# Squared-ReLU attention with a mixture of experts: x's upper parts read in place, whole-pair turns, and a new order of the work around each chunk

## The chip, the cores and the metric

One Trainium2 chip, one of its cores. The time is device microseconds of one launch of the whole program. Engines are called as the profile calls them: PE (TensorE matmuls), PEld (TensorE weight loads), DVE (VectorE), ACT (ScalarE), POOL (GpSimd), SP (SyncE, which issues nearly all DMAs).

## The reference

```python
# u, v: (8, 2496, 256), z: (8, 2496, 64), all float32
attn = np.maximum(z @ z.transpose(0, 2, 1) / 2496, 0.0) ** 2
x = (u * (attn @ v)).reshape(19968, 256)

logits = x @ w_gate                       # 8 experts
expert_idx = np.argmax(logits, axis=1)
probs = np.exp(logits - logits.max(-1, keepdims=True))
probs /= probs.sum(-1, keepdims=True) + 1e-09
gate_w = probs[np.arange(N), expert_idx]
for e in range(8):
    tok_idx = np.where(expert_idx == e)[0]      # at most 80 kept, by gate_w
    h = np.maximum(x[tok_idx] @ w1[e], 0.0)     # 256 -> 1024
    out[tok_idx] = gate_w[tok_idx, None] * (h @ w2[e])
```

The scores are symmetric, so that a block of attn can also be had as the transpose of another one.

## The kernel before

The sequence of each batch is cut into five chunks of 512 queries (the last has 448) and into ten pairs of 128-key tiles. A step is one pair of keys against one chunk of queries: 8 batches x 5 chunks x 10 steps. The loop over steps is written out by hand, and every engine works its own instructions strictly in the order in which the program issues them.

In step r the program issues, in this order: the scores of the pair two steps ahead (`scores`, 6 matmuls L401 into the PSUM tile `s`, of which there is one; then ACT's ReLU L403 out of `s` and ACT's square L404 into the tile `a`, of which there are two); the attention matmuls of the present pair (`attend_pair`, 24 matmuls L439 into `acc`; at step 9 ACT copies the two finished halves of `acc` out, `take` L508); the split of the pair two steps ahead (`split`: an upper part `ah`, cast on ACT L114 or on DVE L116, and a rest `al`, a DVE subtraction reported at the helper's line L58; then DVE turns the pair in blocks of 32 x 32, `mirror` L309, for the mirrored block, which goes out to DRAM as `y` and comes back as `blk`). Where the key block lies before the chunk, no scores are computed: `mirrored` casts `blk` on ACT (L381) and subtracts on DVE. So chunk 0 computes all its ten pairs, and chunk 4 nearly none. The pair on the diagonal is computed by half and turned into `xd` (L346), written as `yd` and read back as `md`.

`acc` has two tiles, one for each half of the 256 columns, and the next chunk's step 0 writes them again.

The finished chunk (`prev`) is worked on during the steps of the next one, in `finished(*prev, r)`. At step 0, `chunk_x` on DVE adds the two halves of the sum and scales them with u (L513). Then x is split into three bf16 parts for the gate's logits: `chunk_hi` (step 1, an ACT cast L518 into `xb`), `chunk_rest` (step 2, DVE), `chunk_mid` (step 3, an ACT cast L526), `chunk_lo` (step 4, DVE). `chunk_store` writes x at step 3 or 4, and `chunk_logits` at step 6 or 7 has 48 small matmuls (L598), each with its weight load out of `xb`; `chunk_sum` adds up their results at the same step. After a batch's last chunk, `gate_top` (step 8: DVE, with the one Exp on ACT, L629, in its middle) and `gate_near` and `gate_sum` (step 9) run in chunk 0 of the next batch.

v is loaded two tiles ahead (`vraw`, two buffers) and split as x is, the upper part by an ACT cast L114 and the rest by a DVE subtraction L143, for the next batch's tiles 0 to 3 at steps 1, 3, 6 and 8 of chunk 4, and for tile 4 at step 3 of the next chunk 0. Weights for the experts come in during the last batch. Behind the last step stands the experts' part.

SP's queue is in program order too. Among its DMAs are `ut` (L150, one buffer, issued at step 2, so that it waits for `chunk_x` of the chunk before), `vraw` (L131), `y`, `blk`, `md`, `xu` (x, L577) and zeros for `out`.

Of the kernel before, what the change touches and what calls it, by code (L numbers as in the profile page):

```python
# [19 lines left out]
P = 128  # L20
# [5 lines left out]
def attn_moe_kernel(ctx, tc, zT, uT, v, wg, w1, w2, out, seq, cap):  # L26
# [15 lines left out]
    QT = 4  # L42
# [83 lines left out]
    def load_v(b, g):  # L126
        last = g == NQ - 1
        nf = QT - 1 if last else QT
        raw = zpool.tile([P, QT, D], F32, tag="vraw", name=f"vraw_{b}_{g}")
        r0 = g * CH  # L130
        nc.sync.dma_start(out=raw[:, :nf],  # L131
                          in_=v[RB[b], r0:r0 + nf * P, :].rearrange("(t p) d -> p t d", p=P))
        if last:

            r1 = r0 + nf * P
            for h in range(2):
                nc.sync.dma_start(out=raw[h * 64:(h + 1) * 64, nf], in_=v[RB[b], r1:r1 + TAIL, :])
        return raw

    def prep_v(b, g, raw, e0, e1):  # L140
        vt = vpool.tile([P, QT, 2, D], F32R, tag="vt", name=f"vt_{b}_{g}")
        cp(e0, vt[:, :, 0], raw)
        e1.tensor_tensor(out=vt[:, :, 1], in0=raw, in1=vt[:, :, 0], op=ALU.subtract)  # L143
        v_t[b, g] = vt

# [357 lines left out]
    def take(b, qc, c):  # L503
# [68 lines left out]
    def chunk_store(b, qc):  # L572
# [37 lines left out]
    def gate_top(b, q0, q1):  # L610
# [363 lines left out]
    def finished(b, qc, r):  # L974

        at_end = b == B - 1 and qc == NQ - 2
        if r == 1:
            chunk_hi(b, qc)
        if r == (1 if at_end else 2):
            chunk_rest(b, qc)  # L980
        if r == (2 if at_end else 3):
            chunk_mid(b, qc)
        if r == (3 if at_end else 4):
            chunk_lo(b, qc)
        if r == (3 if at_end or b >= 2 else 4):
            chunk_store(b, qc)
        if r == (5 if at_end else 6):
            chunk_store2(b, qc)
        if r == (5 if at_end else 6 if qc == NQ - 1 else 7):
            chunk_logits(b, qc)  # L990
            chunk_sum(b, qc)
        if b < B - 1 and qc == NQ - 1:
            if r == 8:
                gate_top(b, 0, NQ)
            elif r == 9:
                gate_sum(b, gate_near(b, 0), gp)
        elif qc == 0 and b > 0:
            if r == 5:
                count(b - 1, 0, BPB, b - 1)
# [3 lines left out]
        elif at_end and r == 7:  # L1003
            gate_top(b, 0, NQ - 1)

    with tc.manual_schedule(engines={ET.PE, ET.Activation, ET.DVE, ET.SP, ET.Pool}):
# [10 lines left out]
        for i, (b, qc, r) in enumerate(steps):  # L1017
# [33 lines left out]
            nb, nqc = (b, qc + 1) if qc + 1 < NQ else (b + 1, 0)  # L1051
            if r == 2:
                prep_u(b, qc)
            if b + 1 < B:
                for j, load, prep in keys_in[qc]:
                    if r == prep:
                        prep_z(b + 1, j, z_raw.pop((b + 1, j)))
                    if r == load:
                        z_raw[b + 1, j] = load_z(b + 1, j)
                if qc == NQ - 2 and r in (2, 4):  # L1060
                    g = r // 2 - 1
                    v_raw[b + 1, g] = load_v(b + 1, g)
                if qc == NQ - 1:
                    if r in (1, 3, 6, 8):
                        g = (1, 3, 6, 8).index(r)
                        prep_v(b + 1, g, v_raw.pop((b + 1, g)), nc.scalar, V)
                        if g + 2 < NQ:
                            v_raw[b + 1, g + 2] = load_v(b + 1, g + 2)
# [490 lines left out]
```

## Time and profile before

| | us |
|---|---|
| Time, median of 3 runs | 1420.04 |
| Lowest and highest | 1419.43 and 1427.58 |
| The profiled execution's own time | 1427.79 |
| Its span, first to last instruction | 1426.1 |

The profiled execution is thus one of the longer ones: 7.75 us above the median, and 1.7 us of it lie around the span. Mean granted TensorE clock: 0.985 of full speed. Busy shares of the span: PE 93%, PEld 76%, DVE 78%, ACT 73%, POOL 3%. A busy time is the union of an engine's instructions; the matmuls' ends are modelled, so that a busy PE can still be a PE at half clock.

### The profile page before, as it was taken

What the parts mean: (1) busy time and instruction counts of PE and PEld (TensorE: products, weight loads), DVE (VectorE), ACT (ScalarE), POOL (GpSimd) and SP (SyncE); (2) the same over time, 40 slices, a digit from 0 to 9 for tenths busy, and PEclk for the clock granted to TensorE, in tenths of its full rate; (3) what the DMA queues carried; (4) which work ended last, traced back from release to release, by engine and by line L of the source; (5) the groups of instructions that cost most, each with busy time, mean ns of one, the idle gap of its engine ahead of it and who ended that gap; (6) DMA issues with size and microseconds to landing.
All of it is one profiled execution on the core that took longest, in us unless ns stands there. A gap on an engine that the chain in (4) does not pass through costs nothing.

```text
span 1426.1 us, 31554 instructions
## 1 busy us (share of the span) xinstructions
PE 1332.9 (93%) x13121; PEld 1086.2 (76%) x13121; DVE 1113.1 (78%) x1531; ACT 1036.0 (73%) x1124; POOL 38.9 (3%) x58
## 2 busy tenths in 40 slices
PE   9999989999899988999999998999999998899997
PEld 6788767887777877878778776787777787787776
DVE  8887788768878788877878678876887768777785
ACT  8875777847777577766877577784777757777765
POOL 0000000000001000000002000000000000000111
PEclk9999999999999999999999999999999999999999
DMA  6898786995878856887567857787479685578764
GB/s 214 275 278 234 219 240 200 234 270 152 234 217 234 235 161 224 228 237 211 190 203 216 244 154 227 213 232 215 137 222 269 188 224 172 189 223 243 196 223 134
DMA packets 192744, 307.02 MB, mean 215 GB/s; under 512 B 35873, under 2 KB 117713, under 8 KB 182353
## 3 DMA queue, kind: packets, MB, share of 16 engines
q1 hardware_dynamic: 191312, 302.62, 72.6%
q0 software_dynamic: 1280, 2.30, 0.6%
q8 instruction: 105, 1.72, 0.5%
q14 instruction: 47, 0.38, 0.1%
HBM read 163.66 MB, written 136.09 MB: 210 GB/s over the span
## 4 chain that ended last, share of the span: by engine, by line
PE 41%; ACT 20%; DVE 17%; DMA 11%; issue 7%; SPq 3%; DVEq 0%; ACTq 0%; POOL 0%; POOLq 0%
PE acc L439 31%; DVE al L58 6%; PE s L401 5%; ACT a L403 5%; ACT a L404 4%; DMA blk<-y 4%; ACT ah L114 3%; DVE x L309 3%; DVE xf L58 3%; DMA y<-x 2%; ACT xf L508 2%; ACT ah L381 2%; PE hp L1286 2%; ACT vt L114 2%; DVE xf L513 1%
## 5 line engine op out<-in xcount | busy, mean ns | idle before, releaser
L439 PE MATMUL acc<-ah,vt 64*128 64x512 f32 (+1 forms) x6240 | 969.3, 387 | 19.8 <-ACT xf L508 19.0
L439 PEld LDWEIGHTS acc<-ah,vt 64*128 64x128 f32 x6240 | 597.6, 186 | 135.1 <-ACT xf L508 30.3
L439 PE MATMUL acc<-al,vt 64*128 64x512 f32 (+1 forms) x3120 | 624.7, 390 | 31.1 <-DVE al L58 30.2
L439 PEld LDWEIGHTS acc<-al,vt 64*128 64x128 f32 x3120 | 305.6, 186 | 105.8 <-DVE al L58 53.2
L58 DVE TENSOR_TENSOR al<-a,ah 128x1024 fp32r<-128x1024 f32 (+1 forms) x240 | 271.8, 1132 | 125.6 <-ACT ah L114 120.5
L403 ACT ACTIVATE a<-s 128x1024 f32<-128x1024 f32 x240 | 229.0, 954 | 120.5 <-PE s L401 117.5
L58 DVE TENSOR_TENSOR al<-blk,ah 128x1024 fp32r<-128x1024 f32 x160 | 193.2, 1219 | 86.3 <-ACT ah L381 86.3
L404 ACT ACTIVATE a<-a 128x1024 f32<-128x1024 f32 x240 | 238.0, 992 | 7.6
L309 DVE STREAM_TRANSPOSE x<-a 128x512 f32<-128x512 f32 x320 | 207.7, 687 | 0.0
L381 ACT CAST ah<-blk 128x1024 fp32r<-128x1024 f32 x160 | 161.2, 1048 | 22.8 <-PE acc L439 12.7
L114 ACT CAST ah<-a 128x1024 fp32r<-128x1024 f32 x153 | 161.0, 1052 | 4.4
L518 ACT CAST xb<-xf 128x1024 bf16<-128x1024 f32 (+1 forms) x39 | 40.1, 1027 | 103.8 <-DVE xf L513 103.5
L508 ACT COPY xf<-acc 128x1024 f32<-128x1024 f32 (+1 forms) x78 | 75.0, 991 | 34.0 <-PE acc L439 32.0
L401 PE MATMUL s<-zh,zh 64*128 64x512 f32 x320 | 66.8, 414 | 28.0 <-ACT a L403 28.0
L401 PE MATMUL s<-zh,zl 64*128 64x512 f32 x480 | 90.3, 372 | 0.0
L401 PE MATMUL s<-zl,zh 64*128 64x512 f32 x480 | 90.0, 370 | 0.0
L116 DVE CAST ah<-a 128x1024 fp32r<-128x1024 f32 (+3 forms) x87 | 49.3, 567 | 34.9 <-ACT a L404 34.6
L401 PEld LDWEIGHTS s<-zh,zh 64*128 64x128 f32 x320 | 30.4, 186 | 44.5 <-ACT a L403 39.4
L526 ACT CAST xb<-xf 128x1024 bf16<-128x1024 f32 (+1 forms) x39 | 40.0, 1026 | 29.3 <-DVE xf L58 29.2
L143 DVE TENSOR_TENSOR vt<-vraw,vt 128x1024 fp32r<-128x1024 f32 x40 | 48.2, 1204 | 13.4 <-ACT vt L114 13.4
L401 PEld LDWEIGHTS s<-zl,zh 64*128 64x128 f32 x480 | 45.6, 185 | 8.3
L401 PEld LDWEIGHTS s<-zh,zl 64*128 64x128 f32 x480 | 45.8, 186 | 5.7
(188 smaller groups left out, 856.3 us busy)
## 6 DMA issues: line engine op xcount, KB each, us to landing
y<-x SPq DMA_DIRECT2D x80, 1024.0 KB
blk<-y SPq DMA_DIRECT2D x320, 256.0 KB
out<-idle SPq DMA_DIRECT2D x40, 512.0 KB
vraw<-v SPq DMA_DIRECT2D x32, 512.0 KB
ut<-uT SPq DMA_DIRECT2D x32, 512.0 KB
wraw<-w SPq DMA_DIRECT2D x30, 512.0 KB
xu<-xf SPq DMA_DIRECT2D x24, 512.0 KB
yd<-xd SPq DMA_DIRECT2D x37, 256.0 KB
```

The source lines that it names most:

```text
L58: V.tensor_tensor(out=o, in0=a, in1=b, op=op)
L114: eng.copy(out=o, in_=i)
L116: eng.tensor_copy(out=o, in_=i)
L143: e1.tensor_tensor(out=vt[:, :, 1], in0=raw, in1=vt[:, :, 0], op=ALU.subtract)
L309: V.transpose(out=x[:, :, :, t].rearrange("p n k s -> p k n s"), in_=a)
L381: nc.scalar.copy(out=natural(ah), in_=src)
L401: nc.tensor.matmul(s[:, h, c0:c1], zk[hs, t * P:(t + 1) * P], zq[hs], start=n == 0, stop=n == 2)
L403: nc.scalar.activation(out=a[:, :, c0:c1], in_=s[:, :, c0:c1], func=AF.Relu)
L404: nc.scalar.activation(out=a[:, :, c0:c1], in_=a[:, :, c0:c1], func=AF.Square)
L439: nc.tensor.matmul(acc_t[b, qc][c][:, h, :nq], v_t[b, k // QT][hs, k % QT, iv, c * P:(c + 1) * P], x[hs, k % 2, :nq], start=at not in begu ...
L508: nc.scalar.copy(out=x[:, :, c], in_=acc_t[b, qc][c][:, :, :x.shape[-1]])
L518: nc.scalar.copy(out=xb[:, 0], in_=xf)
```

## The change

- x's upper parts are no longer cast. A float32 read as two bf16 has its upper half at every second place; `top(x)` is that view. The logits' weight loads and the two subtractions `chunk_rest` and `chunk_lo` read it with a step of two. `chunk_hi` and `chunk_mid` are gone; of the tile `xb` only the third part stays (`xl`).
- `chunk_x` is cut in two: the addition stays at step 0, the scaling moves to step 1 (not in the last chunk). `chunk_rest`, `chunk_lo`, store, rows, logits and sum go to steps 3, 5, 4, 6, 7 and 9 (8 behind a batch's last chunk).
- DVE turns a whole pair (1024 columns) in one instruction in place of two of 512; the diagonal's quarter likewise in one of 512 in place of two of 256.
- The diagonal pairs' casts move from DVE to ACT, except in chunk 0 of each batch.
- `gate_top` moves to step 9 of chunk 0, without the Exp; Exp goes to step 0 of chunk 1, `gate_near` to step 2, the row sums and the reciprocal to step 3, and their four DMAs to step 5.
- v is loaded at steps 2, 3, 5 and 9 of chunk 3 and step 6 of chunk 4, into three buffers; it is cast at step 6 of chunk 3 and steps 3, 5, 7 and 9 of chunk 4, and each subtraction follows one step behind.
- `ut` is loaded at step 4 in place of step 2.

```diff
-    def prep_v(b, g, raw, e0, e1):
+    def prep_vh(b, g, raw, e0):
         vt = vpool.tile([P, QT, 2, D], F32R, tag="vt", name=f"vt_{b}_{g}")
         cp(e0, vt[:, :, 0], raw)
+        v_t[b, g] = vt
+
+    def prep_vl(b, g, raw, e1):
+        vt = v_t[b, g]
         e1.tensor_tensor(out=vt[:, :, 1], in0=raw, in1=vt[:, :, 0], op=ALU.subtract)
...
-        V.transpose(out=x[:, :, :, t].rearrange("p n k s -> p k n s"), in_=a)
-        if t < QT - 1:
+        V.transpose(out=x[:, :, :, t:t + 2].rearrange("p n k t s -> p t k n s"), in_=a)
+        if t < QT - 2:
             return
...
-        on_v = k // QT == qc or (qc, k) in ON_V and b > 0
+        on_v = k // QT == qc and qc == 0 or (qc, k) in ON_V and b > 0
...
+    def top(x):
+        return x.bitcast(BF16)[..., 1::2]
+
     def chunk_tiles(b, qc):
         xf = xpool.tile([P, 2, DC, CH], F32, tag="xf", name=f"xf_{b}_{qc}")
-        xb = xpool.tile([P, 3, DC, CH], BF16, tag="xb", name=f"xb_{b}_{qc}")
+        xl = xpool.tile([P, DC, CH], BF16, tag="xl", name=f"xl_{b}_{qc}")
...
+    def chunk_add(b, qc):
+        x = x_sum[b, qc]
+        tt(x[:, 0], x[:, 0], x[:, 1], ALU.add)
+
     def chunk_x(b, qc):
         x = x_sum.pop((b, qc))
-        tt(x[:, 0], x[:, 0], x[:, 1], ALU.add)
         V.scalar_tensor_tensor(out=x[:, 0], in0=x[:, 0], scalar=CSQ, in1=u_t[b, qc][:, :, :x.shape[-1]],
                                op0=ALU.mult, op1=ALU.mult)
 
-    def chunk_hi(b, qc):
-        xf, xb, _ = xt_t[b, qc]
-        nc.scalar.copy(out=xb[:, 0], in_=xf)
-
     def chunk_rest(b, qc):
-        xf, xb, xr = xt_t[b, qc]
-        tt(xr, xf, xb[:, 0], ALU.subtract)
-
-    def chunk_mid(b, qc):
-        _, xb, xr = xt_t[b, qc]
-        nc.scalar.copy(out=xb[:, 1], in_=xr)
+        xf, xr, _ = xt_t[b, qc]
+        tt(xr, xf, top(xf), ALU.subtract)
 
     def chunk_lo(b, qc):
-        _, xb, xr = xt_t[b, qc]
-        tt(xb[:, 2], xr, xb[:, 1], ALU.subtract)
+        _, xr, xl = xt_t[b, qc]
+        tt(xl, xr, top(xr), ALU.subtract)
...
-                    nc.tensor.matmul(to[:, h, t], xb[hs, i % 3, i // 3, t0:t0 + P], wgs[hs, i // 3],
+                    nc.tensor.matmul(to[:, h, t], xb[i % 3][hs, i // 3, t0:t0 + P], wgs[hs, i // 3],
                                      start=i == 0, stop=i == 3 * DC - 1)
...
+    V_LOAD = [(NQ - 2, 2), (NQ - 2, 3), (NQ - 2, 5), (NQ - 2, 9), (NQ - 1, 6)]
+    V_HIGH = [(NQ - 2, 6), *((NQ - 1, r) for r in (3, 5, 7, 9))]
...
-        if r == 1:
-            chunk_hi(b, qc)
-        if r == (1 if at_end else 2):
+        rest, lo, store, store2, logits, total = (1, 2, 3, 5, 5, 5) if at_end else CHAIN
+        if qc == NQ - 1:
+            logits, total = 7, 8
+        if r == rest:
             chunk_rest(b, qc)
-        if r == (2 if at_end else 3):
-            chunk_mid(b, qc)
...
-        if b < B - 1 and qc == NQ - 1:
-            if r == 8:
-                gate_top(b, 0, NQ)
-            elif r == 9:
-                gate_sum(b, gate_near(b, 0), gp)
+        if b < B - 1 and qc == NQ - 1 and r == 9:
+            gate_top(b, 0, NQ)
         elif qc == 0 and b > 0:
-            if r == 5:
+            if r == 0:
+                gate_exp(b - 1, 0)
+            elif r == 2:
+                ex_t[b - 1] = gate_near(b - 1, 0)
+            elif r == 3:
+                gate_rows(b - 1, ex_t.pop(b - 1), gp, V)
+                gate_recip(b - 1, gp)
+            elif r == 5:
+                gate_store(b - 1)
...
+    CHAIN = 3, 5, 4, 6, 7, 9
...
             if r == 0 and prev:
+                chunk_add(*prev)
+            if r == (0 if last else 1) and prev:
                 chunk_x(*prev)
...
-            if r == 2:
+            if r == 4:
                 prep_u(b, qc)
...
-            if b and qc == 0 and r == 3:
-                prep_v(b, NQ - 1, v_raw.pop((b, NQ - 1)), nc.scalar, V)
+                if (qc, r) in V_HIGH:
+                    g = V_HIGH.index((qc, r))
+                    prep_vh(b + 1, g, v_raw[b + 1, g], nc.scalar)
+            v_low(b, qc, r)
```

## Rows read from the trace of the kernel before

**Rows 1.** Windows, chunks 0, 2, 3: us, PE, PEld, DVE, ACT, POOL, clock, DMA.

```profile
681.83:720.11 38.28, 33.30 (x330) 26.50 (x330) 31.09 (x44) 29.87 (x33) 0.00 (x0) 1.00 0.67 216
...
755.35:787.67 32.32, 32.25 (x328) 26.23 (x328) 25.71 (x42) 25.67 (x27) 10.10 (x8) 1.00 0.79 211
787.67:821.11 33.44, 31.04 (x300) 24.63 (x300) 22.07 (x26) 17.96 (x21) 0.00 (x0) 0.95 0.87 249
```

**Rows 2.** The waits view, whole run: us in total, times, longest us.

```profile
ACT a L403 <- PE s L401: 117.5, 78, 4.0
ACT xb L518 <- DVE xf L513: 103.5, 36, 4.1
...
PE acc L439 <- DVE al L58: 30.2, 40, 2.4
PE s L401 <- ACT a L403: 29.7, 28, 1.5
...
PE acc L439 <- ACT xf L508: 19.0, 16, 2.4
```

**Rows 3.** The timeline of PE in batches 4 and 5: waits in brackets.

```profile
693.31 0.50 PE L401 MATMUL s<-zh,zh 64*128 64x512 f32 x2 [1.48 <-ACT a L403]
...
720.27 0.73 PE L439 MATMUL acc<-ah,vt 64*128 64x512 f32 x4 [2.14 <-ACT xf L508]
...
798.77 0.50 PE L439 MATMUL acc<-al,vt 64*128 64x512 f32 x2 [2.38 <-DVE al L58]
...
837.94 0.47 PE L439 MATMUL acc<-al,vt 64*128 64x448 f32 x2 [0.42 <-DVE al L58]
...
853.99 0.40 PE L401 MATMUL s<-zh,zh 64*128 64x512 f32 x2
```

**Rows 4.** The timeline of ACT in batches 4 and 5.

```profile
691.40 0.94 ACT L518 CAST xb<-xf 128x896 bf16<-128x896 f32 x1 [2.59 <-DVE xf L513]
...
718.86 0.34 ACT L629 ACTIVATE lg<-d 128x160 f32<-128x160 f32 x1 [3.33 <-DVE d L58]
...
852.72 1.04 ACT L403 ACTIVATE a<-s 128x1024 f32<-128x1024 f32 x1
```

**Rows 5.** The timeline of DVE around the starts of chunks 1 and 3.

```profile
719.57 0.32 DVE L636 TENSOR_TENSOR oh<-fw,mf 128x160 bf16<-128x160 f32 x1
...
722.11 1.23 DVE L58 TENSOR_TENSOR al<-blk,ah 128x1024 fp32r<-128x1024 f32 x1 [2.09 <-ACT ah L381]
...
796.36 1.22 DVE L513 SCALAR_TENSOR_TENSOR xf<-xf,ut 128x1024 f32<-128x1024 f32 x1
797.50 1.22 DVE L58 TENSOR_TENSOR al<-blk,ah 128x1024 fp32r<-128x1024 f32 x1
```

**Rows 6.** Windows: first and last of nine at half clock, and one more.

```profile
120.90:124.31 3.41, 3.41 (x20) 2.69 (x18) 2.98 (x3) 1.93 (x3) 0.00 (x0) 0.50 0.94 328
...
1138.07:1141.48 3.41, 3.41 (x18) 2.67 (x16) 2.89 (x3) 1.93 (x3) 0.00 (x0) 0.50 0.95 326
693.00:697.00 4.00, 3.69 (x32) 3.07 (x34) 3.04 (x5) 3.90 (x5) 0.00 (x0) 1.00 0.92 344
```

**Rows 7.** The lines view by shape: count, busy us, mean ns, idle before.

```profile
L309 DVE STREAM_TRANSPOSE x<-a 128x512 f32<-128x512 f32 x320 | 207.7, 687 | 0.0
...
L114 ACT CAST ah<-a 128x1024 fp32r<-128x1024 f32 x153 | 161.0, 1052 | 4.4
...
L518 ACT CAST xb<-xf 128x1024 bf16<-128x1024 f32 x32 | 33.5, 1046 | 85.7 <-DVE xf L513 85.4
...
L116 DVE CAST ah<-a 128x1024 fp32r<-128x1024 f32 x41 | 28.5, 695 | 21.9 <-ACT a L404 21.7
```

**Rows 8.** The timeline of PEld around one chunk's logits: start us, us.

```profile
708.72 0.67 PEld L598 LDWEIGHTS <-xb 64*128 64x128 bf16 x48 [0.26 <-issue]
709.32 0.19 PEld L401 LDWEIGHTS s<-zh 64*128 64x128 f32 x2
709.42 0.19 PEld L401 LDWEIGHTS s<-zh,zl 64*128 64x128 f32 x2
```

More of the change, by code (lines that the diff above doesn't have):

```diff
@@ L128, in load_v @@
         nf = QT - 1 if last else QT
-        raw = zpool.tile([P, QT, D], F32, tag="vraw", name=f"vraw_{b}_{g}")
+        raw = zpool.tile([P, QT, D], F32, tag="vraw", name=f"vraw_{b}_{g}", bufs=3)
         r0 = g * CH
@@ L344, in quarter_out @@
         x = zpool.tile([P, n32, 2, 2, SQ], F32, tag="md", name=f"xd_{b}_{qc}", bufs=1)
-        for t in range(2):
-            V.transpose(out=x[:, :, :, t].rearrange("p n k s -> p k n s"), in_=a[:, t, HQ:])
+        V.transpose(out=x.rearrange("p n k t s -> p t k n s"), in_=a[:, :, HQ:])
         quarter[b, qc] = now[0], x
@@ L423, in split @@
         if k // QT > qc:
-            for h in range(2):
-                mirror(b, k // QT, qc, k % QT + h, a[:, h])
+            mirror(b, k // QT, qc, k % QT, a)
         a_t[b, qc, k] = (ah, al)
@@ L491, in attn_moe_kernel @@
     xt_t, xq_t, lg_t = {}, {}, {}
+    def top(x):
+        return x.bitcast(BF16)[..., 1::2]
     def chunk_tiles(b, qc):
         xf = xpool.tile([P, 2, DC, CH], F32, tag="xf", name=f"xf_{b}_{qc}")
-        xb = xpool.tile([P, 3, DC, CH], BF16, tag="xb", name=f"xb_{b}_{qc}")
+        xl = xpool.tile([P, DC, CH], BF16, tag="xl", name=f"xl_{b}_{qc}")
         nq = min(CH, seq - qc * CH)
-        xt_t[b, qc] = [x[..., :nq] for x in (xf[:, 0], xb, xf[:, 1])]
+        xt_t[b, qc] = [x[..., :nq] for x in (xf[:, 0], xf[:, 1], xl)]
         return xf[..., :nq]
@@ L581, in chunk_store @@
         else:
-            xq = zpool.tile([P, QT * 2 * D], U16, tag="vraw", name=f"xq_{b}_{qc}")
+            xq = zpool.tile([P, QT * 2 * D], U16, tag="vraw", name=f"xq_{b}_{qc}", bufs=3)
             xq_t[b, qc] = x_turn(xf, xq, nq)
@@ L590, in chunk_logits @@
         nq = min(CH, seq - qc * CH)
-        xb = xt_t[b, qc][1]
+        xf, xr, xl = xt_t[b, qc]
+        xb = top(xf), top(xr), xl
         pl = ps_m.tile([P, 2, CH], F32, tag="m", name=f"pl_{b}_{qc}")[:, :, :3 * QT * E]
@@ L628, in gate_top @@
         ex = ex_last[:, q0 * QT:q1 * QT] if last else lg
-        nc.scalar.activation(out=ex, in_=d, func=AF.Exp)
         fw = small("fw")
@@ L641, in gate_top, with gate_exp @@
         gate_t[b, q0] = d, ex, fw
+    def gate_exp(b, q0):
+        d, ex, _ = gate_t[b, q0]
+        nc.scalar.activation(out=ex, in_=d, func=AF.Exp)
     n_gates = [0]
@@ L672, in gate_sum, with gate_recip @@
     def gate_sum(b, ex, pool):
-        col = RB[b] * NT
-        go, g0 = (gt2, b * NT) if b < 2 else (gt, col)
         if b not in sum_t:
             gate_rows(b, ex, pool, V)
+        gate_recip(b, pool)
+        gate_store(b)
+    gq_t = {}
+    def gate_recip(b, pool):
+        col = RB[b] * NT
         V.reciprocal(out=gall[:, col:col + NT], in_=sum_t.pop(b).rearrange("p t o -> p (t o)"))
@@ L680, in gate_sum, with gate_store @@
         V.transpose(out=gq, in_=gall[:, col:col + 32])
+        gq_t[b] = gq
+    def gate_store(b):
+        gq = gq_t.pop(b)
+        go, g0 = (gt2, b * NT) if b < 2 else (gt, RB[b] * NT)
         for g in range(n32):
@@ L856, in load_raw @@
     def load_raw(e, which, part, after=None):
-        pool, tag = (late["raw"], "wraw") if "raw" in late else (zpool, "vraw")
-        raw = pool.tile([P, NPIECE // 2], F32, tag=tag, name=f"wraw_{e}_{which}_{part}")
+        pool, tag, n = (late["raw"], "wraw", None) if "raw" in late else (zpool, "vraw", 3)
+        raw = pool.tile([P, NPIECE // 2], F32, tag=tag, name=f"wraw_{e}_{which}_{part}", bufs=n)
         if after:
@@ L934, in attn_moe_kernel, with v_low @@
     keys_in[NQ - 1] = [(NQ - 2, 1, 4), (NQ - 1, 4, 7)]
+    V_LOAD = [(NQ - 2, 2), (NQ - 2, 3), (NQ - 2, 5), (NQ - 2, 9), (NQ - 1, 6)]
+    V_HIGH = [(NQ - 2, 6), *((NQ - 1, r) for r in (3, 5, 7, 9))]
+    def v_low(b, qc, r):
+        at = (qc, r - 1) if r else ((qc - 1) % NQ, NP - 1)
+        nb = b + 1 if r or qc else b
+        if at in V_HIGH and 0 < nb < B:
+            g = V_HIGH.index(at)
+            prep_vl(nb, g, v_raw.pop((nb, g)), V)
     steps = [(b, qc, r) for b in range(B) for qc in range(NQ) for r in range(NP)]
@@ L1004, in finished @@
             gate_top(b, 0, NQ - 1)
+        elif at_end and r == 8:
+            gate_exp(b, 0)
+    ex_t = {}
+    CHAIN = 3, 5, 4, 6, 7, 9
     with tc.manual_schedule(engines={ET.PE, ET.Activation, ET.DVE, ET.SP, ET.Pool}):
@@ L1059, in attn_moe_kernel @@
                         z_raw[b + 1, j] = load_z(b + 1, j)
-                if qc == NQ - 2 and r in (2, 4):
-                    g = r // 2 - 1
+                if (qc, r) in V_LOAD:
+                    g = V_LOAD.index((qc, r))
                     v_raw[b + 1, g] = load_v(b + 1, g)
[L1063 to L1068, printed above, removed]
-            if b and qc == 0 and r == 3:
-                prep_v(b, NQ - 1, v_raw.pop((b, NQ - 1)), nc.scalar, V)
+                if (qc, r) in V_HIGH:
+                    g = V_HIGH.index((qc, r))
+                    prep_vh(b + 1, g, v_raw[b + 1, g], nc.scalar)
+            v_low(b, qc, r)
             if r == 5 and b < B - 1:
@@ L1100, in attn_moe_kernel @@
         gate_top(b, NQ - 1, NQ)
+        gate_exp(b, NQ - 1)
         gate_near(b, NQ - 1)
```

13 lines of the change are left out of this document (8 added, 5 removed).

## The prediction

> **What bounds the kernel now.** I read the windows of one batch (batch 4) first. In chunk 2 PE is busy for 32.25 of 32.32 us: there the kernel runs at PE's pace. In chunk 0 PE stands still for 5.0 of 38.28 us though neither DVE (31.1) nor ACT (29.9) is full, and in chunk 3 for 2.4 of 33.44 [rows 1]. So the matmuls set the time, and what can be won is PE's waiting. The waits view says for whom [rows 2]: 29.7 us in 28 waits for ACT to empty the one score tile, 19.0 us in 16 waits for ACT to copy `acc` out, 30.2 us in 40 waits for DVE's `al`. The timelines then show the places, which come back in nearly every batch.
>
> (A) In chunk 0, step 3, PE waits 1.48 us [rows 3], because ACT stood for 2.59 us in `chunk_hi`, ahead of the ReLU that frees `s`, until DVE had added and scaled x [rows 4]. Two steps later (B) `chunk_mid` and the cast of v sit ahead of the ReLU, and PE waits nearly as long again. Chunk 1 has up to two shorter waits of the kind (D). (C) At the end of chunk 0 PE waits 2.14 us for `take` [rows 3]: ACT had been held 3.33 us at the Exp, which needs a result of `gate_top` [rows 4]. (E) At the start of chunk 3 PE waits 2.38 us for the `al` of the first mirrored pair [rows 3]; DVE began it at 797.50, right behind the addition and scaling of x [rows 5]. (F) In chunk 4 three waits fall where parts of v and x stand ahead of an `al`; one, of 0.42 us, is shown [rows 3].
>
> Behind the longest of these the clock falls: nine stretches of 3.41 us at 0.50, the 1.2 GHz level, seven behind E and two behind C. Behind the 1.48 us of A it stayed at 1.00 [rows 6]. Each stretch costs half its length, 1.7 us.
>
> **The change part by part.** The sum is made against the profiled execution, 1427.8 us (1426.1 of span and 1.7 around it). It is 7.75 above the median; I take the gain off the median unchanged.
>
> *Upper parts in place.* 78 ACT casts go, 39 at line 518 (32 of them as in [rows 7]) and as many at line 526, some 80 us of ACT. What counts is that ACT no longer stops for DVE, 103.5 us at `chunk_hi` alone [rows 2]. Without these casts and the one of v, the ReLU at A, B and D starts as soon as its scores are there: ACT's own ReLU, square and cast, about 1.05 us each, are 3.1 us a step, and PE's step in chunk 0 is (38.28 - 5.0) / 10 = 3.3 us. Two A-like waits in each of seven batches and twelve D make 26 of the 28; the other two lie in the start and the tail. Gain: 26 / 28 of 29.7, 27.6 us.
>
> What it adds is not in this trace: 32 of the 48 weight loads of each chunk, that is 16 pairs for the two row halves, read bf16 with a step of two. The packed loads follow each other at (709.32 - 708.72) / 24 = 0.025 us a pair, those of four-byte weights at 0.10 (709.32 to 709.42) [rows 8]. Lower end: 0, a gain being excluded since the loads are as many and as wide. Upper end, at the four-byte pace: 16 x 0.075 = 1.2 us a chunk, 47 us in 39 chunks, all on PE's path. I take 0: the row of the same type and width is the nearest. DVE's two subtractions stream a float32 operand beside the bf16 one anyway and take a pass of 1.22 us; 0 there too.
>
> One rule bears on this. The Trainium skill, "TensorE: Matmul & The Clock Gate", section "Weight-path perf modes — Fast Weight Load (FWL) and DoubleRow", says that weights other than fp32 are read 32 bits at a time, two bf16 to a read, and also that the pattern may be packed or strided. By its second half the loads would cost nothing more; by its first each read would bring one wanted value, which is rival 3. No row here shows a strided load.
>
> *Scaling a step later.* At E, DVE's order becomes addition, `al`, scaling, so that 797.50 - 796.36 = 1.14 us leave the path [rows 5]. The diagonal's cast now stands on ACT there (1.05, against 0.70 on DVE [rows 7]), ahead of the two copies and the next pair's cast; the delay of 0.95 meets shorter turns and an idle DVE, and I count it as cancelled, but PE begins the chunk some 0.2 us later for it. So PE waits 2.38 - 1.14 - 0.2 = 1.05 us. Ends: 0.9 with all of the turns' gain, 2.2 with all of ACT's delay. Gain: 7 x 1.33 = 9.3 us.
>
> *Diagonal casts elsewhere* lie in stretches where ACT waits for PE's scores, 117.5 us in 78 waits [rows 2], so 0; without that cover 64 casts of 0.5 to 1.05 us would be some 50 us of ACT.
>
> *Gates a chunk later.* ACT was free at 718.86 - 3.33 = 715.5 [rows 4]; with the diagonal's cast it is free at 716.5. PE ran dry at 720.27 - 2.14 = 718.1 [rows 3] and had finished the first half of `acc` half a step's attention, 1.4 us, earlier, at 716.7. So `take` no longer waits. Gain: 7 x 2.14 = 15.0 us. The first half of the gate, six DVE instructions of up to 0.32 us [rows 5], moves behind the first `al` of chunk 1; before that `al` DVE had 2.09 us idle [rows 5]. Ends: 0 and 7 x 1.8 = 13 us, if the second `al` is late by all of it; I take 0, as PE has a step, 3 us, between the two.
>
> *v sooner.* In chunk 4 the casts and subtractions of v now alternate with those of x, one a step, and the three waits F should go. The 40 waits for `al` without the seven E have (30.2 - 7 x 2.38) / 33 = 0.41 us each; three in seven batches: 8.6 us. The waits behind the two `take`s of chunks 3 and 4 stay. v's last cast moves from step 3 of chunk 0 to the end of chunk 4. It delays by 0.95 the ReLU that ended at 852.72 + 1.04 = 853.76 [rows 4], and PE wanted `s` at 853.99 [rows 3]: a new wait of 0.7 us, 7 x 0.8 with restart, 5.6 us. The subtraction, 1.22 as any pass of this size [rows 5], then stands ahead of DVE's own cast of that chunk's fourth pair, whose `al` may come late by 0 to 1.2; I take half: 7 x 0.6 = 4.2 us.
>
> *Turns.* 160 pairs of turns at 2 x 0.687 [rows 7] become one pass of 1024, 1.22 us like the subtraction of that size [rows 5]: 0.15 each, 24 us of DVE. Lower end 0, if the pass runs as two. It lies beside PE's work; inside E it is counted.
>
> *SP.* `ut` at step 4 no longer holds `md`, `blk` and v behind DVE's scaling, and the third buffer lets v's loads go early. Cost 0, hidden by chunks 2 and 3; if that cover is gone it is rival 2.
>
> *Clock.* With C gone and E at 1.05, under the 1.48 us that the clock survived, the nine drops go: 9 x 1.7 = 15.3 us.
>
> *Restarts.* The first matmuls behind a wait run 0.50 us in place of 0.40 [rows 3]; 26 + 7 + 21 waits at 0.1: 5.4 us.
>
> The sum: 27.6 + 9.3 + 15.0 + 8.6 + 15.3 + 5.4 = 81.2, less 5.6 and 4.2, is 71.4 us. 1427.8 becomes 1356.4; against the median it is **1349 us**.
>
> **The rivals.** (1) *The waits change their name.* ACT is relieved, but DVE, with 31.1 us of work in chunk 0 [rows 1], becomes the late one, and the 27.6 us come back as waits for `al`: 1377. For it: 30.2 us of such waits now. Against it: DVE loses the turns' share, most diagonal casts and half of the gate.
>
> (2) *DMA in chunk 3.* It takes in two more v loads, 1 MB, 4.2 us at 249 GB/s, at a DMA share of 0.87 [rows 1] and in a shorter chunk. If `blk` or `md` came late by that in seven batches: 29 us, 1378. Against it: SP no longer stops there for DVE's scaling.
>
> (3) *Strided loads at half the packed pace*: 16 x 0.025 x 39 = 16 us, 1365. At the four-byte pace of [rows 8]: 47 us, 1396.
>
> (4) *Slower than before: strided loads that don't overlap.* If each pair held PE for the 0.19 us that one four-byte load lasts [rows 8], it would be 16 x 0.165 x 39 = 103 us, 1452. It beats the gain from 71 / (16 x 39) = 0.11 us more a pair. Against it: even the four-byte loads overlap.
>
> (5) *The change doesn't bring what it says*: the pair's turn splits in two, ACT's order around `take` and the ReLU is as tight as before, and the new waits of chunk 0 eat the rest: within 1% of 1420.
>
> **How the numbers follow.** The forecast has 0.56, and its own range is 1332 to 1370: E at 2.2 us would keep its clock drops, 7 x (1.15 + 1.7) = 20 us more; without the new waits and E it would be 17 us less. Rival 1 has 0.13, rival 2 0.08, rival 3 0.07 at 1365 and 0.04 at 1396, rival 4 0.05, rival 5 0.07. A measurement of this kernel tells about 1% from no change. Faster by over 1%: 0.56 + 0.13 + 0.08 + 0.07 + 0.04 = 0.88, of which I give 0.02 to the middle, as 1396 is close to it: 0.86. Within 1%: 0.09. Slower: 0.05. The range goes from 1332 to rival 3's upper end, 1396.
>
> **What would show it.** Mean clock above 0.99 and no stretch at 0.50 before the tail; no ACT wait for DVE's scaling; PE's waits for ACT's ReLU under 10 us in all; chunk 0 near 34.5 us and chunk 3 near 30.4; the 48 loads of a chunk still 0.6 us from the first to the next matmul's. It would be wrong if PE's waits for `al` were above 30 us, if those loads took over 1.5 us, or if ACT waited for `md` or `blk`.

## The result, and the profile after

The changed kernel takes 1366.97 us (median of 4 runs, 1365.26 to 1367.53), the kernel before, run beside it, 1422.67 (1419.43 to 1427.58): a ratio of 0.9604, 95% interval 0.957 to 0.9638. Forecast were 1349 us and a range of 1332 to 1396. The profiled execution after has a span of 1365.2 us and a mean clock of 0.992, against 1426.1 and 0.985. A chunk's span runs here from the start of ACT's second copy of `acc` to the same place of the next chunk.

The windows of the changed kernel that answer to [rows 1], chunks 0, 2 and 3 of batch 4, and under them chunk 2 of batch 1 and a stretch inside it (columns as in [rows 1]):

```profile
661.76:696.25 34.49, 33.33 (x332) 26.80 (x334) 27.78 (x28) 29.11 (x31) 0.00 (x0) 1.00 0.65 208
728.90:761.64 32.74, 32.65 (x330) 26.29 (x327) 24.19 (x35) 25.56 (x27) 10.29 (x8) 1.00 0.84 222
761.64:792.36 30.72, 29.28 (x296) 23.17 (x294) 20.74 (x21) 18.16 (x21) 0.00 (x0) 1.00 0.85 247
238.22:277.56 39.34, 35.71 (x333) 29.72 (x333) 23.38 (x24) 25.99 (x28) 0.00 (x0) 0.91 0.82 208
241.17:248.00 6.83, 6.15 (x29) 4.81 (x31) 2.89 (x4) 1.92 (x3) 0.00 (x0) 0.50 0.37 95
```

Chunk 0 fell from 38.28 to 34.49 us and chunk 3 from 33.44 to 30.72; forecast were 34.5 and 30.4. So in a quiet batch the prediction came true. The fourth line is what it missed: chunk 2 of batch 1 takes 39.34 us where chunk 2 of batch 4 takes 32.74, and 6.83 us of it ran at 0.50, the 1.2 GHz level. In batch 2 it takes 39.46 us, with 3.41 us at 0.50. Together the two are 39.35 + 39.46 - 2 x 32.7 = 13.4 us longer than in a quiet batch; some 1.3 us of it are older, as chunk 2 of batch 2 took 33.65 us before the change and those of quiet batches 32.33.

The waits of the changed kernel that answer to [rows 2], and two more:

```profile
PE acc L444 <- DVE al L58: 17.6, 26, 2.3
PE wp L839 <- DVE lg L609: 7.2, 2, 3.7
PE acc L444 <- ACT xf L516: 5.8, 12, 0.8
PE s L407 <- ACT a L409: 5.5, 8, 1.1
...
DVE zh L122 <- DMA zraw<-zT: 23.3, 14, 4.7
```

PE's waits for the ReLU fell from 29.7 to 5.5 us, those for `take` from 19.0 to 5.8, those for `al` from 30.2 to 17.6; ACT no longer waits for DVE's scaling (103.5 us in [rows 2]). New is the second line, two waits of PE. The last, DVE waiting for the DMA that brings z, was 5.1 us in 3 waits before and is 23.3 in 14.

The two waits of PE, in the timelines of the changed kernel, batch 1, end of chunk 1: ACT, DVE and PE.

```profile
238.22 1.01 ACT L516 COPY xf<-acc 128x1024 f32<-128x1024 f32 x1 [0.34 <-PE acc L444]
239.13 1.05 ACT L387 CAST ah<-blk 128x1024 fp32r<-128x1024 f32 x1
...
237.83 0.71 DVE L352 STREAM_TRANSPOSE xd<-a 128x512 f32<-128x512 f32 x1
240.21 1.23 DVE L58 TENSOR_TENSOR al<-blk,ah 128x1024 fp32r<-128x1024 f32 x1 [1.66 <-ACT ah L387]
241.35 0.35 DVE L609 TENSOR_REDUCE lg<-pl 128x32 f32<-128x192 f32 x1
...
241.85 0.30 PE L839 MATMUL wp<-upper,oh 128*80 128x128 bf16 x1 [3.67 <-DVE lg L609]
```

In batches 1 and 2, step 9 of chunk 1 also issues the matmuls of `blocks` (the call stands in `finished`). They write `wp`, which has the one PSUM tile that the logits' `pl` had, so that they wait until `chunk_sum` (L609) has read `pl`. Before, `chunk_sum` was issued at step 7. Now it too is at step 9, and on DVE's queue it stands behind the `al` of a mirrored pair, which waits for ACT's cast (239.13), which waits behind the two `take`s, which wait for PE's last matmuls of the chunk. PE stood still for 3.67 us, with the next chunk's matmuls queued behind `blocks`.

The rest went as forecast, as far as one can read it line by line. E and two places of the new waits, on PE's timeline in batches 4 and 5:

```profile
771.42 0.50 PE L444 MATMUL acc<-al,vt 64*128 64x512 f32 x2 [1.06 <-DVE al L58]
...
824.01 0.50 PE L407 MATMUL s<-zh,zh 64*128 64x512 f32 x2 [0.57 <-ACT a L409]
...
832.64 0.50 PE L444 MATMUL acc<-al,vt 64*128 64x512 f32 x2 [0.41 <-DVE al L58]
```

E was forecast at 1.05, v's cast ahead of the ReLU at 0.7 (0.8 with restart) and v's subtraction ahead of the fourth pair at 0.6. The strided loads, on PEld's timeline, to be held against [rows 8] (first two, then the first load behind the 48):

```profile
689.89 0.12 PEld L602 LDWEIGHTS <-xf 64*128 64x128 bf16 x4 [0.26 <-issue]
689.94 0.10 PEld L602 LDWEIGHTS <-xl 64*128 64x128 bf16 x2
...
690.49 0.19 PEld L407 LDWEIGHTS s<-zh 64*128 64x128 f32 x2
```

The 48 take 690.49 - 689.89 = 0.60 us, as in [rows 8], and so in each of the 39 chunks: reading with a step of two costs nothing here. Of the rule weighed in the prediction (the Trainium skill, "TensorE: Matmul & The Clock Gate", section "Weight-path perf modes — Fast Weight Load (FWL) and DoubleRow") the trace agrees with the half on packed or strided patterns, and shows nothing of the other half.

### The profile page after: what moved, and what is told of

Read it like the earlier page. It is cut to its first block, busy times and chain, and to the rows that moved or that the text cites. A ratio compares the mean times of both kernels' runs of the same rounds, so it can differ in the third digit from the quotient of the medians.

```text
span 1365.2 us, 31275 instructions
## 1 busy us (share of the span) xinstructions
PE 1314.5 (96%) x13121; PEld 1077.8 (79%) x13121; DVE 1056.5 (77%) x1270; ACT 1018.1 (75%) x1110; POOL 38.5 (3%) x58
## 4 chain that ended last, share of the span: by engine, by line
PE 60%; ACT 11%; DVE 10%; DMA 9%; issue 6%; SPq 3%; DVEq 0%; POOL 0%; ACTq 0%; POOLq 0%
PE acc L444 47%; PE s L407 8%; DVE al L58 3%; ACT a L409 3%; ACT ah L114 3%; ACT a L410 2%; DVE x L316 2%; DMA md<-yd 2%; DMA vraw<-v 2%; PE hp L1322 2%; ACT xf L516 2%; DMA yd<-xd 1%; DVE xf L58 1%; DMA blk<-y 1%; PE pl L602 1%
## 5 line engine op out<-in xcount | busy, mean ns | idle before, releaser
L444 PEld LDWEIGHTS acc<-ah,vt 64*128 64x128 f32 x6240 | 590.8, 185 | 123.0 <-ACT xf L516 19.0
L444 PE MATMUL acc<-al,vt 64*128 64x512 f32 (+1 forms) x3120 | 617.7, 386 | 18.4 <-DVE al L58 17.6
L444 PEld LDWEIGHTS acc<-al,vt 64*128 64x128 f32 x3120 | 302.3, 185 | 89.4 <-DVE al L58 36.6
L114 ACT CAST ah<-a 128x1024 fp32r<-128x1024 f32 (+3 forms) x217 | 213.6, 984 | 5.5
L316 DVE STREAM_TRANSPOSE x<-a 128x1024 f32<-128x1024 f32 x160 | 198.0, 1238 | 0.0
L58 DVE TENSOR_TENSOR xf<-xf 128x1024 f32<-128x1024 f32 (+1 forms) x78 | 91.9, 1178 | 0.0
L58 DVE TENSOR_TENSOR al<-md,ah 128x512 fp32r<-128x512 f32 x37 | 25.1, 679 | 33.6 <-ACT ah L422 33.6
L524 DVE SCALAR_TENSOR_TENSOR xf<-xf,ut 128x1024 f32<-128x1024 f32 (+1 forms) x39 | 46.1, 1181 | 0.0
L58 DVE TENSOR_TENSOR xl<-xf 128x1024 bf16<-128x1024 f32 (+1 forms) x39 | 45.8, 1174 | 0.0
```

Source lines behind the costliest of these rows:

```text
L58: V.tensor_tensor(out=o, in0=a, in1=b, op=op)
L114: eng.copy(out=o, in_=i)
L316: V.transpose(out=x[:, :, :, t:t + 2].rearrange("p n k t s -> p t k n s"), in_=a)
L444: nc.tensor.matmul(acc_t[b, qc][c][:, h, :nq], v_t[b, k // QT][hs, k % QT, iv, c * P:(c + 1) * P], x[hs, k % 2, :nq], start=at not in begu ...
```

## The experiments

Times are medians of 4 or 5 runs, ratios are against the kernel before, run on the same chip; the differences that I name are of medians, and those of ratios lie within some 3 us of them. The theory: the gain comes from reading in place, the later Exp and the later scaling, each at its own waits, and the 18 us that are missing from the forecast lie at `blocks` and at v. The rivals: the new places of the steps brought the gain, or parts of the change share one cover. A span is that of the profiled execution, so that differences of spans and of medians need not be equal.

**sum7.** The sum back at step 7 where `blocks` follows.

```diff
+        if qc == 0 and 0 < b <= 2:
+            total = 7
```

> The changed kernel with one edit: in chunk 1 of batches 1 and 2, chunk_sum stands at step 7 again and not at step 9, where blocks follows it. Theory (the shortfall is one new wait): PE waits 3.67 and 3.58 us at blocks for chunk_sum, which stands on DVE behind the al of a mirrored pair, which waits for ACT's cast behind take; the clock falls after each. Chunk 2 of those two batches goes from 39.4 to 32.7 us: 2 x 6.7 = 13.4 us less, 1353.6 us, 0.951 of the kernel before, and no clock stretch at 0.50 ahead of the tail. Rival (the waits move to the next user of that tile, or the clock falls anyway): less than 4 us.

Measured: 1355.64 us, ratio 0.9531 (0.9502 to 0.956), 11.3 us less. The two waits for L609 are gone from the list; in batch 1 the matmuls of `blocks` now start without a wait, on PE's timeline of this kernel:

```profile
239.42 0.25 PE L839 MATMUL wp<-upper,oh 128*80 128x128 bf16 x1
```

Chunk 2 of the two batches takes 32.83 and 34.20 us, 11.8 less in all. So this cause is shown. One thing came otherwise than expected: a stretch at 0.50 does stand ahead of the tail, 3.41 us behind a wait of 2.37 us for `al` in chunk 4 of batch 0.

**exp_back.** `gate_top` with the Exp in its middle at step 8 of chunk 0.

```diff
+        if not last:
+            nc.scalar.activation(out=ex, in_=d, func=AF.Exp)
...
-        if b < B - 1 and qc == NQ - 1 and r == 9:
+        if b < B - 1 and qc == NQ - 1 and r == 8:
...
-            if r == 0:
-                gate_exp(b - 1, 0)
-            elif r == 2:
+            if r == 2:
```

> The changed kernel with gate_top, Exp included, at step 8 of chunk 0 again; the rest of the gate stays late. Theory (the Exp ahead of take makes C): PE's wait for take comes back at the end of chunk 0, seven times about 2.1 us, with a clock drop of 1.7 us behind some: 15 to 24 us more, 1382 to 1391 us. Rival (ACT is so much freer now that the Exp has cover): within 5 us of 1367.

Measured: 1391.39 us, ratio 0.9798 (0.9763 to 0.9834), 24.4 us more. C is back; its line in the waits of this kernel, and the one behind it on ACT's timeline:

```profile
PE acc L444 <- ACT xf L516: 23.9, 18, 2.8
```

```profile
705.90 0.34 ACT L634 ACTIVATE lg<-d 128x160 f32<-128x160 f32 x1 [2.87 <-DVE d L58]
```

23.9 - 5.8 = 18.1 us are waiting; three stretches of 3.41 us at 0.50, beside those at `blocks` and in the tail, cost half their length, 5.1 us, and are most of the rest. The run doesn't restore the order of before in full: here the sum of the logits stands at step 8, right ahead of `gate_top`, and before it stood at step 6. C's seven waits add up to 18.6 us, and to 14.6 before, so that some 4 of the 24.4 us are more than the change took away.

**scale0.** Addition and scaling both at step 0.

```diff
-            if r == (0 if last else 1) and prev:
+            if r == 0 and prev:
```

> The changed kernel with the addition and the scaling of x both at step 0 again. Theory (the scaling ahead of the al makes E, and a longer E costs the clock too): E's wait goes from 1.06 to about 2.2 us in eight batches and the clock falls behind it again: 8 x 1.15 + 7 x 1.7 = 21 us more, 1388 us. Rival (the whole-pair turns and the in-place parts shortened E, its order doesn't matter): under 4 us more.

Measured: 1384.96 us, ratio 0.9735 (0.9704 to 0.9765), 18.0 us more. E is back at its old length. Two of its seven waits of 2.3 us, and the windows behind them, in this kernel:

```profile
120.02 0.60 PE L444 MATMUL acc<-al,vt 64*128 64x512 f32 x2 [2.29 <-DVE al L58]
...
783.22 0.49 PE L444 MATMUL acc<-al,vt 64*128 64x512 f32 x2 [2.32 <-DVE al L58]
```

```profile
120.28:123.69 3.41, 3.41 (x18) 2.65 (x18) 3.09 (x3) 0.00 (x0) 0.00 (x0) 0.50 0.39 114
783.22:786.63 3.41, 3.41 (x30) 2.82 (x32) 3.35 (x3) 1.02 (x1) 0.00 (x0) 1.00 0.33 86
```

The same wait, and the clock fell behind one and not behind the other: 18 matmuls in 3.41 us there, 30 here. It fell at three of the seven. Chunk 0 grew as well, by 1.1 us a batch: on DVE's timeline addition, scaling and v's last subtraction (679.48 to 681.58) then stand in a row ahead of the next pair's cast (682.71). By spans, 14.4 us of the loss lie in the chunks 3 and 7.1 in the chunks 0, and the chunks 4 give 2.5 back; so the 18.0 are not the price at E alone.

**v_late.** v's casts and subtractions at their old steps, loads at steps 2 and 4 of chunk 3 and 1, 3 and 6 of chunk 4, three buffers kept.

```diff
-    V_LOAD = [(NQ - 2, 2), (NQ - 2, 3), (NQ - 2, 5), (NQ - 2, 9), (NQ - 1, 6)]
-    V_HIGH = [(NQ - 2, 6), *((NQ - 1, r) for r in (3, 5, 7, 9))]
+    V_LOAD = [(NQ - 2, 2), (NQ - 2, 4), (NQ - 1, 1), (NQ - 1, 3), (NQ - 1, 6)]
+    V_HIGH = [(NQ - 1, r) for r in (1, 3, 6, 8)]
...
+        if b and qc == 0 and r == 3:
+            prep_v(b, NQ - 1, v_raw.pop((b, NQ - 1)), nc.scalar, V)
```

> The changed kernel with v's casts and subtractions at their old steps (steps 1, 3, 6, 8 of chunk 4 and step 3 of chunk 0, subtraction right behind the cast) and the loads near their old ones, three buffers kept. Theory (the two places offset each other): the three waits of chunk 4 come back, 7 x 1.1 = 8 us, and the two new waits at the start of chunk 0, 0.57 and 0.41 us and their restarts, go, 7 x 1.3 = 9 us: within 5 us of 1367. Rival (moving v was a plain gain): 8 us or more slower, with the two waits of chunk 0 still there.

Measured: 1351.67 us, ratio 0.9506 (0.9478 to 0.9535): 15.3 us less than the changed kernel. A miss, and the one that taught most: in the sum "v sooner" came out even (8.6 and some 2 of restarts won, 9.8 lost). Chunk 0 of batch 4, to be held against the first line of the windows after:

```profile
649.72:682.78 33.06, 32.91 (x332) 26.88 (x334) 27.78 (x28) 29.03 (x32) 0.00 (x0) 1.00 0.71 220
```

By spans, chunk 0 gives back 10.4 us in seven batches (34.49 to 33.06 each), chunk 4 gives 4.0, all of it in batches 0 to 2, and chunk 2 of batches 1 and 2 gives 2.9. The last is the clock and not v: behind the same two waits at `blocks` it stood at 0.50 for 3.41 us in this execution, and for 10.24 in that of the changed kernel. And in a quiet batch chunk 4 takes 27.88 us as in the changed kernel: the waits F, which were to go with v's new steps, are away without them.

**v4.** Only v's last part goes back to chunk 0, cast at step 3 and subtraction at step 4; the loads stay early.

```diff
-    V_HIGH = [(NQ - 2, 6), *((NQ - 1, r) for r in (3, 5, 7, 9))]
+    V_HIGH = [(NQ - 2, 6), *((NQ - 1, r) for r in (3, 5, 7)), (0, 3)]
...
```

> The changed kernel with only v's last part moved: cast at step 3 of the next chunk 0 and subtraction at step 4, the loads and the first four parts as in the changed kernel. Theory one: both gains of the run with v's old steps hang on this last part (waits at the start of chunk 0, and the late blocks in chunk 4 of batches 0 to 2): about 1352, as that run. Theory two: the late blocks of batches 0 to 2 come from the earlier loads of v, and only the waits at the start of chunk 0 go, 7 x 1.4 us: 1357. Theory three: the waits of chunk 0 move to step 3 and 4 with the cast: 1362 to 1367.

Measured: 1355.98 us, ratio 0.9538 (0.9509 to 0.9566). That is theory two: chunk 0 is down to 33.06 us, but chunk 4 of batches 0 to 2 stays late. One instruction on DVE's timeline, first in this kernel, then in v_late, in batch 0:

```profile
158.37 0.43 DVE L122 CAST zh<-zraw 128x512 fp32r<-128x512 f32 x1 [5.14 <-DMA zraw<-zT]
```

```profile
154.80 0.42 DVE L122 CAST zh<-zraw 128x512 fp32r<-128x512 f32 x1
```

With v's earlier loads DVE stands for 5.14 us before the cast of z, with an `al` behind it, and PE's next wait for `al` is 2.7 us; with the old loads it doesn't stand at all. So the early loads are the likely cause: DVE waits for a DMA, and not for ACT. It isn't shown by itself, as the two kernels also differ in the steps of v's first four casts. Why batches 0 to 2 suffer and 3 to 7 don't stays open. One difference lies in SP's queue, which in batches 0 and 1 also issues DMA transposes of x (one pair takes 6.37 us of it, at 128.22 in the changed kernel); but batch 2 has them in its first chunk alone, and v_late has them too.

**in_place.** The kernel before, with the upper parts read in place and nothing else.

```diff
+    def top(x):
+        return x.bitcast(BF16)[..., 1::2]
...
-    def chunk_hi(b, qc):
-        xf, xb, _ = xt_t[b, qc]
-        nc.scalar.copy(out=xb[:, 0], in_=xf)
...
-        tt(xr, xf, xb[:, 0], ALU.subtract)
+        tt(xr, xf, top(xf), ALU.subtract)
...
```

> The kernel before with only the upper parts read in place: the two casts of x on ACT are gone, every other step stays where it was. My theory takes the 29.7 us of PE's waits for ACT's ReLU and their restarts (2.6 us) away and leaves the waits for `take` and for the first mirrored `al`, with their nine clock drops, where they are: about 1390 us, ratio 0.979 against the kernel before. Rival one (the casts were harmless, the new places of the steps brought the gain): above 1410. Rival two (the casts also stood behind the waits for `al` in chunk 4, so that these go as well): 1376 to 1382. Strided loads that cost something would show as loads of a chunk's logits over 0.60 us.

Measured: 1382.61 us, ratio 0.9723 (0.9697 to 0.9749), 39.7 us less than the kernel before. That is rival two, just above its range. Its waits of PE for the ReLU and for `al`, to be held against [rows 2]:

```profile
PE acc L439 <- DVE al L58: 24.0, 24, 2.4
...
PE s L401 <- ACT a L403: 4.2, 9, 1.1
```

The windows of chunks 1 and 4 of batch 4, first in the kernel before, then in this one:

```profile
720.11:755.35 35.24, 34.83 (x336) 29.11 (x338) 28.82 (x44) 28.08 (x31) 0.00 (x0) 0.95 0.65 202
821.11:851.01 29.90, 28.20 (x306) 23.73 (x302) 24.85 (x28) 21.01 (x24) 0.00 (x0) 1.00 0.56 167
```

```profile
695.96:729.04 33.08, 32.93 (x336) 26.93 (x338) 28.71 (x45) 26.34 (x29) 0.00 (x0) 1.00 0.73 224
793.90:822.04 28.14, 27.48 (x306) 23.95 (x302) 24.80 (x29) 19.41 (x22) 0.00 (x0) 1.00 0.62 184
```

Chunk 0 gives 14.3 and chunk 1 13.6 us in seven batches, chunk 4 14.9 in eight. Chunk 3 gives 3.9, which is the clock: in this execution it fell behind E in four of seven batches and behind C in one, in the profiled one of before in seven and two. In chunk 4 DVE has the same work as before (24.85 and 24.80 us), v stands where it stood, and still PE stands for 28.14 - 27.48 = 0.66 us in place of 1.70. How, is seen in chunk 4 of the kernel before, on ACT's and then on DVE's timeline, and under it in the same place of this kernel:

```profile
827.94 1.05 ACT L518 CAST xb<-xf 128x1024 bf16<-128x1024 f32 x1 [2.98 <-DVE xf L513]
828.89 1.05 ACT L114 CAST vt<-vraw 128x1024 fp32r<-128x1024 f32 x1
...
829.97 1.23 DVE L143 TENSOR_TENSOR vt<-vraw,vt 128x1024 fp32r<-128x1024 f32 x1 [0.98 <-ACT vt L114]
831.12 1.22 DVE L58 TENSOR_TENSOR al<-blk,ah 128x1024 fp32r<-128x1024 f32 x1
```

```profile
801.69 1.22 DVE L143 TENSOR_TENSOR vt<-vraw,vt 128x1024 fp32r<-128x1024 f32 x1
```

ACT stood for DVE in `chunk_hi`, its cast of v came late behind that, and DVE stood for the cast of v, with an `al` behind it. This wait of DVE, 13.4 us in 14 places before, is gone from the list of this kernel; it fell twice in each chunk 4.

**half_turns.** Each pair turned in two halves again.

```diff
-        V.transpose(out=x[:, :, :, t:t + 2].rearrange("p n k t s -> p t k n s"), in_=a)
+        for h in range(2):
+            V.transpose(out=x[:, :, :, t + h].rearrange("p n k s -> p k n s"), in_=a[:, h])
...
```

> The changed kernel with each pair turned by two instructions of 512 columns again, and the quarter by two of 256. DVE gets 160 x (2 x 0.687 - 1.238) = 22 us more work. Theory: it lies beside PE's work but for the starts of chunk 3, where the wait for `al` of 1.06 us grows by one or two such pairs, 0.14 to 0.28 us, without a clock drop: 1367 to 1372. Rival: that wait passes the point where the clock falls, seven drops of 1.7 us: 1380 to 1385.

Measured: 1367.73 us, ratio 0.9621 (0.9601 to 0.9642): no difference. E is 1.12 us in place of 1.06. The 22 us of DVE's work lay beside PE's, as the theory said.

**diag_v.** The diagonal casts on DVE again.

```diff
-        on_v = k // QT == qc and qc == 0 or (qc, k) in ON_V and b > 0
+        on_v = k // QT == qc or (qc, k) in ON_V and b > 0
```

> The changed kernel with the diagonal pairs' casts on DVE again in every chunk. Theory (the move cost and brought nothing, as the prediction counted it): within 5 us of 1367. Rival one: ACT is relieved ahead of the two copies of `acc` and of the first mirrored cast at the starts of chunks 1 to 3, so that the wait of 1.06 us at chunk 3 gets shorter and the late sum ahead of the block counts with it: 1350 to 1360. Rival two: DVE's extra 0.7 us stand ahead of the diagonal's `al` and of the mirrored ones, and PE waits there: 1372 to 1385.

Measured: 1361.47 us, ratio 0.9575 (0.9555 to 0.9596), 5.5 us less (4.1 by the ratios, whose intervals overlap those of the changed kernel): just outside the theory, towards rival one, and hardly clear of noise. But E, which was to get shorter by that rival, is the same. What got shorter is chunk 2, by 0.36 us in a quiet batch (32.38 for 32.74) and by some 1 us on average in batches 1 and 2, where half of the stretch at 0.50 in batch 1 is gone too, 1.7 us that are the clock's; all eight give 4.0 us, and chunk 4 1.3, most of it in the last batch.

**three_back** undoes the three losses together: the edits of sum7, v_late and diag_v.

> The changed kernel with three of its parts undone together: the sum back at step 7 in chunk 1 of batches 1 and 2, v's casts and loads at their old steps, the diagonal casts on DVE. What stays of the change is the reading in place, the later scaling and gates, and the pair turns. Theory (the three cost separately, at separate places): v's old steps alone gave 1351.7, less 11 for the sum, less 4 for the casts: 1337. Rival (they share one cover, so that the second and third bring less): 1343 to 1348.

Measured: 1336.67 us, ratio 0.9386 (0.9362 to 0.941). Less 11.3, 15.3 and 5.5 us the changed kernel would be at 1334.9: the three add up to within 2 us, and the rival's 1343 to 1348 is out.

**three_add1** goes on from there:

```diff
-            if r == 0 and prev:
-                chunk_add(*prev)
             if r == (0 if last else 1) and prev:
+                chunk_add(*prev)
+            if r == (0 if last else 2) and prev:
                 chunk_x(*prev)
```

> The same, with x's addition at step 1 and its scaling at step 2, one step later each. Theory: at the starts of chunk 3 the first mirrored `al` no longer stands behind the addition, which takes the wait of 1.06 us and its restart away in eight batches, 9 us: 1328. Rival: what is then late there is ACT's cast for that `al`, behind the two copies of `acc`, and the wait keeps most of its length: 1335 to 1337; or the parts of x, now closer together, make an `al` late in another chunk: above 1337.

Measured: 1329.28 us (1328.41 to 1329.51), ratio 0.9335 (0.9312 to 0.9358), the fastest version here. PE's waits for `al` are down to 3.9 us, none over 0.7. On DVE's timeline at the start of chunk 3 the mirrored `al` now stands ahead of the addition, and PE's windows of batch 4 (chunks 0 to 4) are nearly full:

```profile
740.00 1.24 DVE L316 STREAM_TRANSPOSE x<-a 128x1024 f32<-128x1024 f32 x1
741.16 1.18 DVE L58 TENSOR_TENSOR al<-blk,ah 128x1024 fp32r<-128x1024 f32 x1
742.26 1.22 DVE L58 TENSOR_TENSOR xf<-xf 128x1024 f32<-128x1024 f32 x1
```

```profile
635.39:668.30 32.91, 32.75 (x332) 26.95 (x334) 28.61 (x30) 28.07 (x30) 0.00 (x0) 1.00 0.64 201
668.30:701.39 33.09, 33.09 (x336) 26.55 (x336) 29.59 (x44) 26.52 (x29) 0.00 (x0) 1.00 0.72 227
701.39:733.76 32.37, 32.26 (x328) 26.26 (x326) 24.95 (x36) 24.08 (x26) 10.24 (x8) 1.00 0.90 244
733.76:763.09 29.33, 29.33 (x300) 23.46 (x300) 21.42 (x23) 16.06 (x18) 0.00 (x0) 1.00 0.90 263
763.09:790.97 27.88, 27.24 (x306) 23.99 (x304) 24.53 (x27) 19.31 (x22) 0.00 (x0) 1.00 0.68 207
```

## Why the prediction was right, and where it was not

The direction, the size to within 1.3%, and the mechanism held: PE's waits bound the kernel, and the change took most of them away. The forecast is 18.3 us too low. Of these, 7.8 lie in the step from the profiled execution to the median, and the other 10.5 in the sum: the spans differ by 1426.1 - 1365.2 = 60.9 us, where it said 71.4. By place: chunks 0 and 1 gave 44.1 us for some 39 in the sum, chunk 3 20.5 for some 21, chunk 4 10.9 for 10.7; chunk 2, for which the sum has nothing, lost 14.6. So the shortfall lies in chunk 2 alone.

- **Upper parts in place**: right in kind, too small. 27.6 and some 2.6 for restarts were in the sum; the run alone gave 39.7, as F went with it. The strided loads cost 0, as taken.
- **v sooner** was put to the wrong cause. The gain of 8.6 us at F was booked here because parts of v and x stood ahead of those `al`s; in_place shows that F belongs to ACT's casts of x, which held up ACT's casts of v. That chunk 4 came out as forecast is thus luck: the gain is there, but not by v's new steps. What was truly v's own, the two new waits in chunk 0, was forecast at 5.6 + 4.2 = 9.8 us and measured 10.4. So v sooner is a loss, 15.3 us with what came with its loads and with 2.9 of the clock; and **SP**, where the early loads were taken at 0, has the rest of it, the 4.0 us in chunk 4 of batches 0 to 2.
- **A step that was moved and not weighed**: `chunk_sum` from step 7 to 9, where `blocks` waits for it. The sum has no term for it; undoing it gave 11.3 us, 11.8 by the spans of chunk 2. The code could have shown the danger: `blocks` in step 9 writes the one buffer out of which `chunk_sum` reads.
- **Gates a chunk later**: 15.0 and, with two clock drops and the restarts, 19 us were forecast, 24.4 measured, some 4 of them by the order in that run. Scaling a step later: 9.3 and, with seven drops and the restarts, 22 against 18.0, of which a part lies in chunk 0, where the scaling met v's subtraction. E at 1.06 us hit the forecast of 1.05, but 0.2 us of that are luck: they were put to the diagonal's cast on ACT, and with that cast back on DVE (diag_v) E is 1.03 to 1.07.
- **Diagonal casts elsewhere** were counted at 0 and cost some 4 us, hardly clear of noise. **Turns** at 0: right.
- **Clock**: the nine drops went, as forecast, but 10.24 us at 0.50 came at `blocks`, so that the sign "no stretch before the tail" failed. And nine was a trait of the profiled execution. In 23 other executions of the kernel before, the span goes with the clock, from 1417.5 us at 0.994 to 1425.9 at 0.985; the profiled one, at 0.985, stands at the long end. A median execution had fewer drops to lose, so that the gain off the median is smaller than off the profile by those 7.8 us.
- **Rivals**: 1 did not come, `al` waits fell to 17.6 us. 2 came small: chunk 4 of batches 0 to 2 is 30.45 + 28.76 + 29.05 - 3 x 27.87 = 4.7 us late, not 29, and ACT's waits for `md` rose from 11.0 to 21.5 us, and 8.9 us in 5 waits for `blk` are new. By the prediction's own words that was a sign of being wrong; the sign was badly chosen, as ACT waited for `md` before as well. 3, 4 and 5 are out.

The single terms, 39.7 + 24.4 + 18.0, less 11.3, 15.3 and 5.5, make 50.0 us; the whole change gives 55.7. The 5.7 us between them are not traced. Part of it is the clock at `blocks`, which stands in the loss of more than one run (2.9 us in v_late, 1.7 in diag_v).

## What to carry to other kernels

Before a wait is put down to the instruction that stands ahead of the late one on its own engine, follow the late one's input too: F looked like DVE's queue and began on ACT's. For each step that is moved, look at what the other engines issue in the step that it moves to, and at which single buffers the two share. And a term for the clock counts against the profiled execution, not against the median, when the two differ in clock.

## What the runs showed of the hardware that was not expected

The clock's fall is not settled by the length of a wait. At E, in waits of 2.3 to 2.4 us at the same place or right behind them, it fell in seven of seven batches of the kernel before, in four of in_place and in three of scale0. Behind the two waits at `blocks`, 3.67 and 3.58 us, it stayed at 0.50 for 6.83 and 3.41 us in the changed kernel, and in v_late for 3.41 us and not at all. Behind the waits of 1.03 to 1.12 us at E's place, in the changed kernel and in half_turns, no stretch at 0.50 followed. What decides stays open.

Nor does each fall cost the 1.7 us of the prediction. In scale0 it nearly does: chunk 3 takes 33.34 us with one (batch 0) and 31.75 without (batch 4). But behind C, in the kernel before, it cost nothing. Chunk 1 of batch 4, with a fall, takes 35.24 us (the first window under in_place); that of batch 5 has none and takes as long:

```profile
889.14:924.39 35.25, 33.55 (x336) 26.78 (x338) 28.84 (x45) 28.08 (x30) 0.00 (x0) 1.00 0.66 199
```

PE is busy there for 33.55 us in place of 34.83, and waits for ACT's ReLU instead, 0.90 and 0.64 us, where batch 4 has one such wait of 0.25. There ACT set the pace in either case.
